# Fused attention and two mixture products on one core: a planner that orders the stage, and a power of two moved onto x

## The chip, the cores and the metric

The kernel runs on one core of a Trainium2 chip. The metric is the device time of one execution in microseconds (us); all times here are microseconds unless marked ns. The engines are PE (matrix products, with PEld for the loading of its weights), DVE (vector), ACT (activations), POOL (GpSimd) and SP (which issues most transfers). "Clock" is the clock that was granted to PE, as a share of its 2.4 GHz.

## What is computed

Causal attention on 2 batches x 12 heads, 448 positions, width 64; its output, laid out as 896 tokens x 768, goes through a gated product (w_a and w_b 768 x 1536, w_out 1536 x 768) and then through one of eight experts per token (768 x 1024 x 768):

```python
scores = scale * np.matmul(q, k.transpose(0, 1, 3, 2))
mask = np.triu(np.ones((seq, seq), dtype=bool), k=1)
scores = np.where(mask, -1000000000.0, scores)
scores = scores - np.max(scores, axis=-1, keepdims=True)
attn = np.exp(scores)
attn = attn / (np.sum(attn, axis=-1, keepdims=True) + 1e-09)
return np.matmul(attn, v).astype(np.float32)
...
x = np.ascontiguousarray(attn_out.transpose(0, 2, 1, 3)).reshape(B * S, H * D)
...
a = x @ w_a
b = x @ w_b
return (a * b @ w_out).astype(np.float32)
...
logits = xn @ en.T / tau
expert_idx = np.argmax(logits, axis=1)
...
h = np.maximum(x[mask] @ w1[e], 0.0)
out[mask] = gate_w[mask, None] * (h @ w2[e])
```

## The kernel before

Heads are taken in twelve pairs (six per batch, `pairs`). Of a pair the scores come in three units (`UNITS`: rows 336 to 447, rows 112 to 223, and the other two chunks), and five steps (`SUBS`) turn them into products with V. Of each step `exps` (L373, ACT) makes the exponentials and their sums from the scores and the maxima (`maxima`, L357, DVE), `turn` (L382, PE) transposes the probabilities, `p_hi` (L385, ACT) and `p_lo` (L388, DVE) split them into two float16 halves in one of `NTB = 3` buffers `tbuf`, and `pv` (L404 to L406, PE) multiplies them by V's halves. After a pair `inverse` (L415) and `weigh` (L428, DVE) divide by the sums into x0, and then `turn_x` (L449, PE) and `halves_x` (L455 ACT, L457 DVE) make the pair's part of x's halves. `prep` scales K and V on POOL (L304, L307), copies V's high half on ACT (L310) and makes its low half on POOL (L313).

The weights arrive as float64. A conversion makes one block of 128 x 768 into two float16 halves: `a`, `b`, `c` (L218, L222, L226, DVE), `e` (L232, ACT) and `d` (L236, DVE); there are 24 blocks of w_a and w_b and 12 of w_out, the first eight of them in attention. A block of w_out is also transposed by a transfer (`we_turn`) and multiplied with the embedding on PE (`we_mm`, L615 and L616).

The first product (`gemm1_steps`, L517 to L519) goes in units of one block f of 128 columns and one batch hf: 18 matmuls of 448 columns for a and 18 for b, 24 units, 864 matmuls. The result of a is multiplied on DVE by `rows` (L525), then by b (L529); ACT makes the high half of g (L530), POOL the low one (L531). `rows` is a power of two per token, made from the squared norms of x0 (`squares`, `norm`), spread over the partitions by a product with ones (`spread`, L495) and copied (L498). The second product (L839) follows.

What sets the order: each engine runs its instructions in program order, and the program is written by a list of tasks, each put at a step and with a rank inside it:

```python
    def at(step, rank, fn):
        lst = tasks.setdefault(max(step, clock[0]), [])
        lst.append((rank, len(lst), fn))
...
    for g in range(NU):
        at(S0 + g, 3, lambda g=g: exps(g))
        at(S0 + g + 1, 1, lambda g=g: turn(g))
        at(S0 + g + 1, 3.2, lambda g=g: p_hi(g))
        at(S0 + g + 2, 1.5, lambda g=g: p_lo(g))
        at(S0 + g + 2, 8, lambda g=g: pv(g))
    for s in range(S0 + 5 * NSB, S0 + NU):
        at(s, 9, lambda s=s: fill(FILL))
    FILL = 3
    for s in range(S0 + NU):
        if s < 4 or s % 5 in (0, 2):
            at(s, 9.3, tick)
```

Step g thus has its exponentials in one slot, its transposes and high half in the next, its low half and its products in the one after; within a slot the rank decides. `fill` writes up to three times three matmuls of the first product, if the conversion and the part of x that they need have been written, and `tick` one instruction of a conversion. The loads of a pair (`load`) are written two pairs ahead, those of the weights (`more_raw`) one after each conversion, all on SP's queue. The units that `fill` could reach are those of blocks 0 to 3 with batch 0 and of block 0 with batch 1; the others come after attention, in the same way by steps, with one instruction of a conversion to two groups of three matmuls.

## Time and profile before

| | us |
|---|---|
| runs before: median (lowest to highest of 3) | 672.51 (669.19 to 676.47) |
| the profiled execution, its own time | 676.15 |
| its span, first to last instruction | 674.4 |
| PE busy over the span | 570.2 (85%) |
| DVE, ACT, POOL busy | 416.9 (62%), 202.5 (30%), 153.0 (23%) |

All durations come from that one profiled execution. Matmuls are pipelined and their ends are modelled, so a matmul's own duration is longer than its share of PE: what a row of matmuls costs is read from the starts. "Idle before" is the time for which an engine had nothing to run before such an instruction, with what ended it.

### The profile page before, as it was taken

The numbers are of one execution on the slowest core, as the hardware profiler recorded it, in microseconds if no ns is written. First come the engines' busy times: TensorE is split into PE (matmuls) and PEld (weight loads), VectorE is DVE, ScalarE is ACT, GpSimd is POOL, SyncE is SP. The second block draws the span as 40 slices with busy tenths as digits, with TensorE's granted clock in tenths as the row PEclk, the third lists the DMA queues.
The fourth block names the chain that finished last, engine by engine and source line by source line (L and its number), as shares of the span: only waits on it lengthen the run. The fifth ranks groups of instructions, "written<-read, shape, count | busy, mean of one in ns | idle before, by whom it ended". The sixth has DMA issues, their size and how long they took to land. (4 is left out here: it accounts for less than half of the span.)

```text
span 674.4 us, 12613 instructions
## 1 busy us (share of the span) xinstructions
PE 570.2 (85%) x5102; PEld 378.8 (56%) x5102; DVE 416.9 (62%) x643; ACT 202.5 (30%) x465; POOL 153.0 (23%) x134
## 2 busy tenths in 40 slices
PE   2767787787988699999998599999599879998994
PEld 1545554454655355455544266665588675957772
DVE  3865555634455389877998506888448974959100
ACT  2554445523446322222222100110312133322221
POOL 5422222202331022121111000000133334334222
PEclk9976566578979699999999699999999999999998
DMA  8430321202010056524799303988487884857111
GB/s 303 156 104 15 96 81 40 89 28 88 15 48 1 1 80 204 185 93 134 186 256 199 70 2 133 319 299 286 105 193 219 296 264 129 273 181 243 39 34 29
DMA packets 46230, 93.04 MB, mean 138 GB/s; under 512 B 23430, under 2 KB 26502, under 8 KB 46160
## 3 DMA queue, kind: packets, MB, share of 16 engines
q1 hardware_dynamic: 43872, 84.16, 41.8%
q0 software_dynamic: 2288, 7.91, 3.5%
q8 instruction: 48, 0.79, 0.5%
q14 instruction: 22, 0.18, 0.1%
HBM read 79.46 MB, written 9.05 MB: 131 GB/s over the span
## 5 line engine op out<-in xcount | busy, mean ns | idle before, releaser
L517 PE MATMUL ab<-bufA 128*128 128x448 f16 x288 | 105.3, 365 | 9.6 <-DVE asb L525 4.9
L518 PE MATMUL ab<-bufA 128*128 128x448 f16 x288 | 105.6, 366 | 0.0
L519 PE MATMUL ab<-bufA 128*128 128x448 f16 x288 | 105.4, 366 | 0.0
L357 DVE TENSOR_REDUCE mn<-sc 112x2 f32<-112x896 f32 (+3 forms) x48 | 34.4, 737 | 65.6 <-PE sc L346 65.6
L382 PE MATMUL pt<-id,pr 112*112 112x112 f32 x240 | 44.8, 325 | 32.3 <-DVE tbuf L388 16.5
L839 PE MATMUL x<-woc,gL 128*128 128x512 f16 x336 | 57.4, 326 | 0.0
L385 ACT ACTIVATE tbuf<-pt 112x448 f16<-112x448 f32 x60 | 32.6, 543 | 79.7 <-PE pt L382 68.0
L373 ACT ACTIVATE pr<-sc,mn 112x336 f32<-112x336 f32 (+2 forms) x96 | 46.6, 492 | 26.5 <-DVE mn L357 20.7
L382 PEld LDWEIGHTS pt<-id,pr 112*112 112x112 f32 x240 | 32.2, 168 | 39.2 <-issue 27.3
L340 PE MATMUL sc<-ld,ld 64*112 64x448 f32 (+3 forms) x192 | 45.2, 582 | 5.8 <-POOL ld L304 5.8
L518 PEld LDWEIGHTS <-bufA 128*128 128x128 f16 x288 | 28.9, 100 | 36.1 <-issue 14.0
L519 PEld LDWEIGHTS <-bufA 128*128 128x128 f16 x288 | 29.1, 101 | 28.6 <-issue 3.6
L388 DVE TENSOR_TENSOR tbuf<-pt,tbuf 112x448 f16<-112x448 f32 x60 | 36.7, 612 | 11.6 <-ACT tbuf L385 11.6
L839 PEld LDWEIGHTS <-gL 128*128 128x128 f16 x336 | 32.1, 98 | 20.5
L517 PEld LDWEIGHTS <-bufA 128*128 128x128 f16 x288 | 29.1, 101 | 25.2 <-issue 2.8
L406 PE MATMUL po<-vh,tbuf 112*128 112x64 f16 x240 | 34.9, 216 | 9.4 <-DVE tbuf L388 7.4
L531 POOL TENSOR_TENSOR gL<-asb,gL 128x448 f16<-128x448 f32 x16 | 20.6, 1290 | 94.6 <-ACT gL L530 94.6
L1041 PEld LDWEIGHTS <-hh 128*128 128x128 f16 x320 | 30.9, 98 | 19.8
L226 DVE SCALAR_TENSOR_TENSOR cv<-raw,cv 128x768 uint32<-128x768 uint32 x36 | 40.9, 1136 | 0.5
L222 DVE SCALAR_TENSOR_TENSOR cv<-raw,cv 128x768 uint32<-128x768 uint32 x36 | 37.7, 1047 | 0.7
L313 POOL TENSOR_TENSOR vl<-ld,vh 112x512 f16<-112x512 f32 x12 | 15.1, 1259 | 95.7 <-ACT vh L310 95.7
L404 PE MATMUL po<-vh,tbuf 112*128 112x64 f16 x240 | 36.7, 219 | 0.1
(229 smaller groups left out, 1388.1 us busy)
## 6 DMA issues: line engine op xcount, KB each, us to landing
rw<-in_moe_w_dram SPq DMA_DIRECT2D x36, 512.0 KB, 6.2
rw<-in_moe_w_dram SPq DMA_DIRECT2D x48, 384.0 KB, 5.3
raw<-in_moe_w_a_dram SPq DMA_DIRECT2D x12, 768.0 KB, 7.2
raw<-in_moe_w_b_dram SPq DMA_DIRECT2D x12, 768.0 KB, 6.4
raw<-in_moe_w_out_dram SPq DMA_DIRECT2D x12, 768.0 KB, 4.7
ld<-in_k_dram SPq DMA_DIRECT2D x12, 224.0 KB, 2.5
ld<-in_q_dram SPq DMA_DIRECT2D x12, 224.0 KB, 2.8
ld<-in_v_dram SPq DMA_DIRECT2D x12, 224.0 KB, 2.5
```

Of the source, the lines that this page charges most:

```text
L222: nc.vector.scalar_tensor_tensor(t, r()[:, :, 1], 0xC0000000, t, op0=ALU.bitwise_and, op1=ALU.bitwise_or)
L226: nc.vector.scalar_tensor_tensor(t, r()[:, :, 0], 29, t, op0=ALU.logical_shift_right, op1=ALU.bitwise_or)
L340: nc.tensor.matmul(sc[:CP, j, o : o + W], qt[hd, c * CP : W], kt[hd, :W], start=n == 0, stop=False)
L373: nc.scalar.activation(pr[:, d : d + W], sc[:CP, jj, o : o + W], AF.Exp, bias=mn[:, c, jj : jj + 1], scale=-1.0, accum_out=sums[pi][:, c, ...
L382: nc.tensor.transpose(pt[:CP, cs], prs[g][:, cs], id32[:CP, :CP])
L388: nc.vector.tensor_tensor(tbufs[g % NTB][:, 1, :S], pts.pop(g)[:CP, :S], tbufs[g % NTB][:, 0, :S], op=ALU.subtract)
L404: nc.tensor.matmul(po[:, c, jj, :], ph, vh[:, kc, jj, :], start=kc == 0, stop=False)
L406: nc.tensor.matmul(po[:, c, jj, :], pl_, vh[:, kc, jj, :], start=False, stop=kc == c)
L517: nc.tensor.matmul(o, w[:, 0, i, kc, :], xTh[:, kc, ts], start=kc == 0, stop=False)
L518: nc.tensor.matmul(o, w[:, 0, i, kc, :], xTl[:, kc, ts], start=False, stop=False)
L519: nc.tensor.matmul(o, w[:, 1, i, kc, :], xTh[:, kc, ts], start=False, stop=kc == KC - 1)
L839: nc.tensor.matmul(xp[:, ns], G(f)[:, a, tk], woc[:, f, l, ns], start=st, stop=sp)
```

## The change

The list of steps is replaced by a planner (`Plan`). Each piece of work becomes an `op` with an engine, an estimated duration, the pieces that it needs and a rank. The planner keeps an estimated clock for each engine; it picks, for the engine that can start first, the piece of lowest rank among those that can start within a small slack, adds its estimated duration, and writes the instruction. The kernel holds the order that comes out; nothing is decided while it runs. It covers all from the first K to the last block of w_out; the 36 matmuls of a unit are now single pieces of rank 5000, after everything in attention.

The power of two per token no longer comes in as `rows`. `norm` makes it as before from the squares of x0, now for exponents in steps of two, and `x_scale` multiplies x0 by it, two chunks on ACT and two on DVE, when all six pairs of a batch are weighed. Only then is x turned, six times for a batch in a row (`turn_x` by batch and block), instead of once after every pair. Gone are `rows`, its product with ones, its copy, and the multiplication by it: `g_a` is now a scaled copy on ACT. `g_lo` moves from POOL to DVE, `v_hi` from ACT to POOL, the first half of the reciprocal (`inverse`) from DVE to POOL, pair 0's K scaling from POOL to DVE. Buffers: probabilities and `tbuf` four instead of three, conversions three instead of two, x0 two instead of one. Only pair 0's loads stand ahead of the set-up now. The first eight conversions wait, in the plan, for the exponentials of steps 20, 25, ... 55, so that the first stands in the fifth pair.

```diff
+class Plan:
+    SLACK = {"PE": 0.1, "DVE": 0.2, "ACT": 0.1, "POOL": 0.0, "SP": 0.0}
+    LAT = {"PE": 0.3, "DVE": 0.17, "ACT": 0.2, "POOL": 0.2, "SP": 2.2}
...
+    def pick(self, eng):
+        t, best = self.free[eng], None
+        for o in self.wait[eng]:
+            r = t
+            for d in o.deps:
+                if d.end is None:
+                    break
+                r = max(r, d.end + (d.lat if d.eng != eng else 0.0))
+            else:
+                key = (0, o.rank, r) if r <= t + self.SLACK[eng] else (1, r, o.rank)
+                if best is None or key < best[0]:
+                    best = (key, r, o)
+        return best
...
+        oa = op("DVE", 0.6, a, ld, old(NCV, 5), after, rank=k)
...
+        eng = nc.vector if pi == 0 else nc.gpsimd
+        eng.tensor_scalar(ldt[pi, 1], ldt[pi, 1], SQ, None, op0=ALU.mult)
...
+        nc.gpsimd.tensor_copy(vf(qkv[pi][0]), vf(ldt[pi, 2]))
...
-        nc.vector.tensor_scalar(rs, rs, 1e-9, SV, op0=ALU.add, op1=ALU.mult)
+        nc.gpsimd.tensor_scalar(rs, rs, 1e-9, SV, op0=ALU.add, op1=ALU.mult)
...
+    def x_scale(b, c):
+        x0 = x0s[b][:, c, :]
+        if c % 2:
+            nc.vector.tensor_scalar(x0, x0, r2[b][:, c : c + 1], None, op0=ALU.mult)
+        else:
+            nc.scalar.activation(x0, x0, AF.Copy, scale=r2[b][:, c : c + 1])
...
-                at(c + 1, 1.8, lambda: nc.vector.tensor_tensor(asb, rows[:, hf, :], o, op=ALU.mult))
...
-                at(c + 2, 4, lambda: nc.gpsimd.tensor_tensor(G(f)[:, 1, ts], asb, G(f)[:, 0, ts], op=ALU.subtract))
...
+        nc.scalar.activation(asb, gt[0][:, :S], AF.Copy, scale=ACU)
...
+        nc.vector.tensor_tensor(G(f)[:, 1, ts], gt.pop(("a", f, hf)), G(f)[:, 0, ts], op=ALU.subtract)
...
+    for i, fn in enumerate(emb_tasks):
+        emb_o = op("DVE", 0.2, fn, emb_o, rank=12 + 0.01 * i)
...
+                t_o[g] = op("PE", 0.4, lambda g=g: turn(g), e_o[g], l_o.get(g - 2), rank=g + 0.5)
+                h = op("ACT", ACTC(S), lambda g=g: p_hi(g), t_o[g], v_o.get(g - NTB), rank=g + 0.6)
+                l_o[g] = op("DVE", DVEC(S), lambda g=g: p_lo(g), h, rank=g + 0.6)
+                v_o[g] = op("PE", 0.37, lambda g=g: pv(g), l_o[g], vl_o[pi], wg_o.get(pi - 1), v_o.get(g - 1), rank=g + 1.5)
...
+                    prev_mm[0] = op("PE", 0.189, lambda f=f, hf=hf, i=i, kc=kc, n=n: mm(f, hf, i, kc, n), *deps, rank=5000)
...
+    for n in range(NC1):
+        conv_ops(n, after=e_o[C1A + C1B * n])
...
+    for f in range(NF):
+        conv_ops(2 * NF + f)
+        to = op("SP", 2.0, lambda f=f: we_turn(f), conv[2 * NF + f][5], we_o.get(f - NWT), rank=400)
+        we_o[f] = op("PE", 0.4, lambda f=f: we_mm(f), to, rank=400)
```

How the order of the instructions changes is shown at three places. The first is the start of DVE's queue: cv is a block under conversion, mn the maxima, gE and esm the embedding and its norms. Before:

```order
L137 CAST idb<-id_96 112x112
L139 CAST id_103<-id_96 128x128
L218 TENSOR_SCALAR cv_170<-raw_168 128x768
L222 SCALAR_TENSOR_TENSOR cv_170<-raw_168,cv_170 128x768
L226 SCALAR_TENSOR_TENSOR cv_170<-raw_168,cv_170 128x768
L357 TENSOR_REDUCE mn_184<-sc_179 112x2
L218 TENSOR_SCALAR cv_191<-raw_172 128x768
L236 SCALAR_TENSOR_TENSOR bufA<-cv_170,bufA 128x768
```

After, the last steps of the embedding's chain, which starts DVE's queue, and what stands behind it:

```order
L299 TENSOR_SCALAR esm<-esm 8x1
L302 TENSOR_SCALAR esm<-esm 8x1
L303 RECIPROCAL esm<-esm 8x1
L333 TENSOR_SCALAR ld_0_84<-ld_0_84 128x448
L304 TENSOR_SCALAR gE<-gE,esm 8x768
L305 RECIPROCAL rtau<-rtau 128x1
L378 TENSOR_REDUCE mn_174<-sc_159 112x2
L378 TENSOR_REDUCE mn_174<-sc_169 112x2
```

The conversion that stood ahead of the first maxima is gone, and the whole chain on the embedding, with the scaling of pair 0's K (ld_0) in it, stands there now.

The second place is DVE in the fifth pair before (pt are transposed probabilities, x_0 the output of batch 0, px turned x):

```order
L415 TENSOR_SCALAR sums_668<-sums_668 112x8
L420 RECIPROCAL rr_843<-sums_668 112x8
L218 TENSOR_SCALAR cv_858<-raw_189 128x768
L388 TENSOR_TENSOR tbuf_115<-pt_826,tbuf_115 112x448
L428 TENSOR_TENSOR x_0_390<-po_744,rr_843 112x4x128
L388 TENSOR_TENSOR tbuf_117<-pt_860,tbuf_117 112x448
L357 TENSOR_REDUCE mn_779<-sc_891 112x2 x2
L222 SCALAR_TENSOR_TENSOR cv_858<-raw_189,cv_858 128x768
L388 TENSOR_TENSOR tbuf_113<-pt_884,tbuf_113 112x448
L357 TENSOR_REDUCE mn_941<-sc_931 112x2
L457 SCALAR_TENSOR_TENSOR bufA<-px_919,bufA 128x448
```

and in the fourth and fifth pair after:

```order
L378 TENSOR_REDUCE mn_729<-sc_750 112x2
L409 TENSOR_TENSOR tbuf_111<-pt_745,tbuf_111 112x448
L258 TENSOR_SCALAR cv_797<-raw_192 128x768
L262 SCALAR_TENSOR_TENSOR cv_797<-raw_192,cv_797 128x768
L409 TENSOR_TENSOR tbuf_113<-pt_778,tbuf_113 112x448
L378 TENSOR_REDUCE mn_729<-sc_788 112x2 x2
L409 TENSOR_TENSOR tbuf_107<-pt_815,tbuf_107 112x448
L447 TENSOR_TENSOR x_0_395<-po_709,rr_761 112x4x128
L378 TENSOR_REDUCE mn_862<-sc_821 112x2
L409 TENSOR_TENSOR tbuf_109<-pt_844,tbuf_109 112x448
L409 TENSOR_TENSOR tbuf_111<-pt_856,tbuf_111 112x448
```

The low halves of turned x (L457) no longer stand among a pair's work, the first half of the reciprocal (L415) has gone to POOL, and the first conversion begins here.

The third place is PE after the last product with V (pn is the spread row factor, ab a result of the first product). Before:

```order
L406 LDWEIGHTS tbuf_117
L406 MATMUL po_2214<-vh_165,tbuf_117 128x64
L449 MATMUL px_2322<-id_96,x_1_1418 128x112 x4
L495 LDWEIGHTS onesb
L495 MATMUL pn_2339<-dg_142,onesb 128x112
```

After:

```order
L507 LDWEIGHTS bufA
L507 MATMUL ab_2151<-bufA 128x448
L461 MATMUL px_2174<-id_90,x_1_1358 128x112 x8
L461 MATMUL px_2185<-id_90,x_1_1358 128x112 x8
L507 LDWEIGHTS bufA
```

Before, the turned x and the row factor follow at once on the last product with V, and then come 705 matmuls of the first product. After, 29 of its matmuls stand between that product and the turned x, and 796 behind them; 39 stand ahead of it, where 159 stood.

## Rows read from the trace of the kernel before

**Rows 1.** Busy time by stage: width, busy (instructions) of PE, PEld, DVE, ACT, POOL; clock; DMA

```profile
14.82:116.34 101.52, 75.79 (x672) 52.84 (x673) 62.70 (x116) 52.06 (x158) 29.16 (x21) 0.75 0.28 89
116.34:224.10 107.76, 88.81 (x779) 58.51 (x777) 55.34 (x104) 49.80 (x148) 21.13 (x16) 0.81 0.13 42
224.10:236.60 12.50, 7.56 (x31) 3.26 (x28) 3.73 (x12) 2.18 (x8) 0.00 (x0) 0.59 0.01 1
236.60:375.80 139.20, 134.07 (x806) 70.03 (x805) 122.06 (x149) 33.69 (x47) 26.95 (x21) 1.00 0.62 165
```

**Rows 2.** In order of time, three places: start, duration, engine, line, names, idle before

```profile
14.82 0.62 ACT L373 ACTIVATE pr<-sc,mn 112x448 f32<-112x448 f32 x1
...
224.08 0.19 PE L406 MATMUL po<-vh,tbuf 112*128 112x64 f16 x1
...
384.17 5.29 PE L839 MATMUL x<-woc,gE 128*128 128x512 f16 x24
```

**Rows 3.** Groups of DVE until 240: busy, mean ns, idle before and who ended it

```profile
L388 DVE TENSOR_TENSOR tbuf<-pt,tbuf 112x448 f16<-112x448 f32 x60 | 36.7, 612 | 11.6 <-ACT tbuf L385 11.6
L357 DVE TENSOR_REDUCE mn<-sc 112x2 f32<-112x896 f32 (+3 forms) x48 | 34.4, 737 | 65.6 <-PE sc L346 65.6
```

**Rows 4.** PE in order of time, 199.6 to 201.9

```profile
199.64 0.55 PE L382 MATMUL pt<-id,pr 112*112 112x112 f32 x4
200.11 1.02 PE L340 MATMUL sc<-ld,ld 64*112 64x336 f32 x8
...
201.31 0.19 PE L404 MATMUL po<-vh,tbuf 112*128 112x64 f16 x1
...
201.66 0.36 PE L517 MATMUL ab<-bufA 128*128 128x448 f16 x1
201.85 0.35 PE L518 MATMUL ab<-bufA 128*128 128x448 f16 x1
```

**Rows 5.** PE in order of time, 73.7 to 76.6

```profile
73.72 0.26 PE L404 MATMUL po<-vh,tbuf 112*128 112x64 f16 x1
...
74.38 0.97 PE L382 MATMUL pt<-id,pr 112*112 112x112 f32 x4
75.28 1.09 PE L340 MATMUL sc<-ld,ld 64*112 64x224 f32 x4
...
76.53 0.26 PE L404 MATMUL po<-vh,tbuf 112*128 112x64 f16 x1
```

**Rows 6.** In order of time: the transfer and first step of the embedding

```profile
2.99 0.75 POOL L176 DMA_DIRECT2D gE<-in_moe_expert_emb_dram  x1
...
15.78 1.91 DVE L261 SCALAR_TENSOR_TENSOR gE<-gE 8x768 f32<-8x768 f32 x1
```

**Rows 7.** DMA issues: KB each, median us from issue to landing

```profile
gE<-in_moe_expert_emb_dram POOLq DMA_DIRECT2D x1, 24.0 KB, 6.0
```

**Rows 8.** Lines of the conversion: duration ns min/median/max, first and last start

```profile
L218 DVE TENSOR_SCALAR cv<-raw x36: 506/550/1424, 11.0 to 373.1; 128x768 uint32<-128x768 uint32 x36
...
L222 DVE SCALAR_TENSOR_TENSOR cv<-raw,cv x36: 906/959/1794, 11.6 to 375.5; 128x768 uint32<-128x768 uint32 x36
...
L226 DVE SCALAR_TENSOR_TENSOR cv<-raw,cv x36: 906/951/1676, 12.6 to 376.5; 128x768 uint32<-128x768 uint32 x36
...
L236 DVE SCALAR_TENSOR_TENSOR bufA<-cv,bufA x24: 934/950/1782, 14.9 to 323.7; 128x768 f16<-128x768 f32 x24
```

**Rows 9.** Groups of PE from 224.1 to 384.1

```profile
L517 PE MATMUL ab<-bufA 128*128 128x448 f16 x235 | 84.1, 358 | 1.2 <-DVE asb L525 1.1
L615 PE MATMUL pW<-en,woT 128*128 128x16 f16 x71 | 5.1, 171 | 12.1 <-DMA woT<-woc 12.1
```

**Rows 10.** In order of time: a POOL subtraction and a conversion beside it

```profile
238.87 1.67 POOL L531 TENSOR_TENSOR gE<-asb,gE 128x448 f16<-128x448 f32 x1 [27.16 <-ACT gE L530]
...
239.68 1.67 DVE L226 SCALAR_TENSOR_TENSOR cv<-raw,cv 128x768 uint32<-128x768 uint32 x1
```

**Rows 11.** Groups of DVE in the dense stage, 236.6 to 375.8

```profile
L226 DVE SCALAR_TENSOR_TENSOR cv<-raw,cv 128x768 uint32<-128x768 uint32 x27 | 31.4, 1165 | 0.4
```

More of the change, by code (lines that the diff above doesn't have):

```diff
@@ L128, in load @@
         ldt[pi, i] = t
-    for pi in range(2):
-        for i in (1, 0, 2):
-            load(pi, i)
+    for i in (1, 0, 2):
+        load(0, i)
     id32 = cst.tile([P, P], F32, name="id32")
@@ L236, in d @@
             nc.vector.scalar_tensor_tensor(lo, st["t"].bitcast(F32), SW, hi, op0=ALU.mult, op1=ALU.subtract)
[L237 to L254 removed]
+        old = lambda k, i: conv[n - k][i] if n >= k else None
+        k = 1000 + n
+        ld = op("SP", 2.6, lambda: ab_raw(n), old(NRAW, 3), old(1, 0), rank=k)
+        oa = op("DVE", 0.6, a, ld, old(NCV, 5), after, rank=k)
+        ob = op("DVE", 0.88, b, oa, rank=k)
+        oc = op("DVE", 0.88, c, ob, rank=k)
+        oe = op("ACT", 0.75, e, oc, *dest_free, rank=k)
+        od = op("DVE", 0.88, d, oe, rank=k - 0.5)
+        conv[n] = (ld, oa, ob, oc, oe, od)
     esm = cst.tile([E, 4], F32, name="esm")
@@ L433, in weigh @@
-        at(s0 + 1, 4.7, lambda: halves_x(pi, 1))
-        if hp >= NPR - 2:
-            part = hp - NPR + 2
-            for c in range(NCH):
-                at(s0 + 1 + (0 if part else c), 5.2, lambda c=c: squares(b, c, part))
-        if hp == NPR - 1:
-            at(s0 + 2, 5, lambda: norm(b))
-            at(s0 + 3, 9.2, lambda: spread(b))
-            at(s0 + 4, 3.5, lambda: spread_done(b))
-    pxs = {}
-    def turn_x(pi):
-        b, hp = pairs[pi]
-        pxs[pi] = pt = psA.tile([P, 512], F32, tag="pt", name=f"px{pi}", bufs=2)
-        for c in range(NCH):
-            nc.tensor.transpose(pt[:, c * CP : (c + 1) * CP], x0s[b][:, c, 2 * hp * D : (2 * hp + 2) * D], id32[:CP, :CP])
@@ new lines, in ACTC, with DVEC, last @@
+    def ACTC(n):
+        return 0.09 + 0.00084 * n
+    def DVEC(n):
+        return 0.08 + 0.00104 * n
+    ld_, sc_o, e_o, t_o, v_o, l_o, x_o = {}, {}, {}, {}, {}, {}, {}
+    ac_free, sc_free = [], []
+    def last(lst, k):
+        return lst[-k] if len(lst) >= k else ()
+    emb_o = None
+    for i, fn in enumerate(emb_tasks):
+        emb_o = op("DVE", 0.2, fn, emb_o, rank=12 + 0.01 * i)
+    eo = op("PE", 0.5, emb_turn, emb_o, rank=13)
+    eh = op("ACT", 0.3, emb_hi, eo, rank=13)
+    el = op("DVE", 0.25, emb_lo, eh, rank=13)
@@ new lines, in fused_kernel @@
+    seq = [(f, hf) for hf in range(2) for f in range(4)] + [(f, hf) for f in range(4, NF) for hf in range(2)]
+    for n in range(NC1):
+        conv_ops(n, after=e_o[C1A + C1B * n])
+    for f in range(NFIRST):
+        unit(f, 0)
+    plan.run(needed)
+    begun = [x for x in unit_o if unit_o[x][0].end is not None]
+    for x in unit_o:
+        if x not in begun:
+            plan.drop(unit_o[x])
+    plan.run([o for x in begun for o in unit_o[x]])
+    prev_mm[0] = mm_o[begun[-1]] if begun else None
@@ L585, in fused_kernel @@
+    prev_lo[:] = [unit_o[x][-1] for x in begun]
     psx.close()
@@ L618, in fused_kernel @@
     wo_buf["c"] = woc
-    steps = []
-    for f in range(1, 4):
-        steps += gemm1_steps(f, 1)
-    for f in range(4, NF):
-        steps += gemm1_steps(f, 0) + gemm1_steps(f, 1)
-    for n in range(0, len(steps), 2):
-        for st in steps[n : n + 2]:
-            at(clock[0], 6, st[1])
-        if n % 12 != 10:
-            at(clock[0], 9, lambda n=n: tick())
-        run_step()
-    while conv:
-        at(clock[0], 9, tick)
-        run_step()
-    while tasks and max(tasks) >= clock[0]:
-        run_step()
+    del ac_free[:]
+    for f, hf in seq[len(begun) :]:
+        for i in range(2):
+            if 2 * f + i not in conv:
+                conv_ops(2 * f + i, mm_o[f - NS, 1] if f >= NS else None)
+        unit(f, hf)
+    we_o = {}
+    for f in range(NF):
+        conv_ops(2 * NF + f)
+        to = op("SP", 2.0, lambda f=f: we_turn(f), conv[2 * NF + f][5], we_o.get(f - NWT), rank=400)
+        we_o[f] = op("PE", 0.4, lambda f=f: we_mm(f), to, rank=400)
+    plan.run([o for e in plan.wait for o in plan.wait[e]])
     cvs.close()
```

329 lines of the change are left out of this document (161 added, 168 removed).

## The prediction

> **What bounds the kernel now.** I read the busy time by stage first, then the groups of the attention stage, then PE in order of time. By stage the span splits into attention (first scores of exponentials at 14.82 to the last product with V at 224.1), a short join, the dense first product, a tail, and the second product from 384.17 on, which the change leaves alone [rows 1, 2]. In attention no engine is full: PE shows 76 and 89 of 102 and 108 us, DVE 63 and 55, ACT 52 and 50 [rows 1]. The time goes into engines waiting for each other: the maxima on DVE waited 65.6 us for PE's scores [rows 3]. The twelve pairs of heads took (224.1 - 14.82) / 12 = 17.4 us each. PE's granted clock was 0.75 and 0.81 there, that is, it went between its two levels. The dense stage is PE's: 134 of 139 us at clock 1.00 [rows 1].
>
> What a pair costs PE when nothing waits is read from starts in a row. At the higher level (2.4 GHz): four transposes 0.47 (199.64 to 200.11), scores of the third unit 1.20 (200.11 to 201.31), a product with V 0.35 (201.31 to 201.66) [rows 4]; the first unit has as many columns with half the mask matmuls, an estimated 1.1. At the lower level (1.2 GHz): product 0.66, transposes 0.90, scores of the second unit 1.25 [rows 5]; the first two are about 1.85 times the higher level's, so the second unit is some 0.70 there. A pair is 5 x 0.47 + 1.20 + 1.1 + 0.70 + 5 x 0.35 = 7.1 us at the higher level and 7.1 x 1.85 = 13.1 at the lower.
>
> **The change, part by part.**
>
> *Start.* The K scaling of pair 0 goes from POOL to DVE, and there it stands behind the whole chain on the expert embedding. That chain waits for a transfer that POOL issues at 2.99 [rows 6] and that lands 6.0 us later [rows 7], at about 9.0. Behind it are queued the scaling, and for it PE's first scores, and the first maxima. Sum: 9.0 + 1.9 for the squares of the embedding [rows 6] + 14 small steps at an estimated 0.17 + 0.5 for the scaling + 2.2 for the first scores (1.20 x 1.85) + 1.1 for the maxima = 17.1 instead of 14.82: 2.3 us lost. If the squares take less and the transfer lands at 7, it is nothing; if the transfer is delayed by the other loads, 5.
>
> *Attention, pairs 0 to 3.* The conversions now begin with the twenty-first step (pair 4), and the turned x with pair 6. DVE has left per pair 34.4 / 12 = 2.9 for maxima, 5 x 0.612 for the low halves [rows 3], and an estimated 0.9 for weighing and reciprocal: 6.9 us. ACT had 52.06 / 6 = 8.7 per pair [rows 1] and loses V's copy (to POOL) and x's half, each an activation of some 0.6 like the one at 14.82 [rows 2]: about 7.5. PE needs 7.1 or 13.1. So no engine needs more than 7.5 at the higher level, and PE alone sets 13.1 at the lower. The planner's order is what fills the waits: instead of one fixed slot per step an engine gets whatever is ready by estimate, and four buffers stand behind the probabilities and their halves instead of three. I take 10.1, the middle between 7.1 and 13.1, since the granted clock before was itself midway (0.75).
>
> *Attention, pairs 4 to 11.* Eight conversions fall here, one per pair. Alone one is 0.51 + 0.91 + 0.91 + 0.95 = 3.3 us on DVE by the shortest instances [rows 8]. To 6.9 + 3.3 come about 1.0 per pair for six low halves of x, its scaling, the norms and one and a half units of the first product: 11.2. PE at the lower level needs 13.1 + (six turned x at 0.9 + 39 matmuls at 2 x 0.189) / 8 = 15.6. The middle is 13.4. V's high half on POOL costs POOL at most another 1.6 per pair (what a POOL instruction of that shape takes is bounded by its other two, nothing at the low end if ACT was the tighter); POOL was busy 29.2 / 6 = 4.9 of 17 per pair [rows 1], so it fits. The reciprocal's first half now waits in POOL's queue too, behind such an instruction for 0 to 1.6 us, and the weighing, and with it the next pair's products, wait with it; four buffers cover this, so I take 0 and leave 12 x 1.6 = 19 in the upper end. On SP the weights' loads stand between the pairs' loads, each behind an earlier conversion; three Ks and Qs are loaded ahead, which hides that. The last product with V then comes at 17.1 + 4 x 10.1 + 8 x 13.4 = 164.7 instead of 224.1.
>
> *First product.* By the order 159 of its 864 matmuls stood before the last product with V, leaving 705 (235 at each of three lines) [rows 9]; now 39 do, leaving 825, so 120 more at the 0.189 that two starts in a row show (201.66, 201.85) [rows 4]: 22.7 us that before lay inside attention. 825 x 0.189 = 155.9. With it 24 turned x (6 x 0.47 = 2.8) and twelve small products with the turned output weights at about 0.3 (3.6): 162.3. The join shrinks: before, PE did 7.6 us of work in 12.5 at clock 0.59 [rows 1]; now 29 matmuls of the first batch (5.5 us) stand between the last product with V and the first turned x, beside weighing, squares, norm and scaling (0.7 + 2 + 0.9 + 1.7 = 5.3 estimated from the like instructions). So the row factor's broadcast and its waits go, and nothing new shows if the units run ready; if not, 5 us.
>
> *DVE and POOL in the dense stage.* The row factor's multiplication goes to ACT as a scaled copy, the low half of g comes from POOL to DVE: two DVE instructions per unit as before. But the conversions get quicker. Beside a POOL subtraction of 1.67 one of them took 1.67 [rows 10], where the shortest took 0.91 and the median 0.95 [rows 8]. The mean in this stretch was 1.17 [rows 11]; with no POOL work beside, 28 conversions at 3.4 and 23 units at 1.2 are 123 us of DVE in 162: PE stays the bound. The Trainium skill says why in "SBUF — State Buffer", section "Who interferes with whom": a DVE instruction with two SBUF inputs and a GpSimd one that reads SBUF block each other for the whole instruction. The trace agrees (1.67 against 0.91); by that rule the gain is DVE's alone here and the sum stays, while V's copies on POOL give some of it back in attention.
>
> *Tail.* Before, PE waited 12.1 us for turned output weights, mostly after its last unit [rows 9]. Now 42 matmuls (7.9 us) stand behind the last of these small products. Conversion and transfer of the twelve blocks go one behind another; before they came 4.8 us apart, and DVE needs 3.4 + 0.8 now. I take 6 of the 12.1 us as left, and 2 us for the change of the PSUM pool; ends 0 and 15. Dense stage: 162.3 + 8 = 170.3, against 384.17 - 224.1 = 160.1.
>
> **Sum.** Second product from 164.7 + 170.3 = 335.0 instead of 384.2: 49 us earlier. The rest of the span (290 us) keeps its instructions. The profiled execution took 676.15 us (span 674.4), 3.6 above the median of the runs shown, 672.5; 676.15 - 49 = 627, and on the median's footing 672.5 - 49 = 623.5, which I round to 624.
>
> A rule that speaks against it: the Trainium skill, "Perfetto Trace Analysis", section "Optimization Strategy", says that stages with different limits may gain by being interleaved, and this change takes 120 matmuls out of such a mixture. The trace bears it out in part: the second batch held most of the 159 and took only 6.2 us longer than the first [rows 1]. By that the sum would be some 18 us better had they stayed; it holds their full 22.7.
>
> **The rivals.**
> *PE at its lower level all through attention.* For it: with transposes, narrow products and waits the clock of 0.75 came about although PE showed 75 to 82% busy [rows 1]. Against it: the waits that the planner closes are PE's. Time: 17.1 + 4 x 13.1 + 8 x 15.6 = 194.3, the second product at 364.6, 652 us. Chance 0.18.
> *PE at its higher level, DVE and ACT bound.* 17.1 + 4 x 7.5 + 8 x 11.2 = 136.7; with the dense stage without waits at 162.3 + 2, second product at 301, 589 us. For it: in the stretch of [rows 4] PE ran without a gap at that level. Chance 0.17.
> *Slower: the order is fixed by estimates, and one late engine holds all.* The place is PE's queue in attention: a transpose whose exponentials are late stands ahead of everything else. If a pair takes 17.4 us as now, the last product with V comes at 226, the 120 matmuls come on top, second product at 396, 684 us. It decides from (384.2 - 170.3 - 17.1) / 12 = 16.4 us a pair. For it: estimated durations that hold at the higher level only. Against it: even all of attention at the lower level is 14.8. Chance 0.10, of which slower by over 1% 0.06.
> Mine, the mixture: 0.55.
>
> **How the numbers follow.** The time is the mixture's 624. Its own range is 605 to 642; to both sides it reaches to the rivals, leaving half of each out: 597 to 654. One per cent is about what a measurement here can tell from no change. Faster by more: 0.55 + 0.17 + 0.17 of the lower level's 0.18 = 0.89; within: 0.05; slower: 0.06.
>
> **What would show it.** Right: first exponentials near 17; a pair every 10, then 13 us; granted clock above 0.8 in attention; the last product with V near 165; PE without a gap at 0.189 a matmul after that; conversions at 0.91 to 0.96; the second product near 335. Wrong: pairs of over 16 us, or PE waiting for DVE in the dense stage for more than 15 us in all, or the first exponentials after 22.

## The result, and the profile after

The changed kernel takes 585.81 us (median of 4 runs, 585.13 to 586.54) against 670.85 for the kernel before (median of 4, 669.1 to 676.47) in the same session: 0.872 of the time, 95% interval 0.8664 to 0.8776. The forecast was 624 with a range of 597 to 654, so the time lies 38 us below the forecast and 11 below the range. It is the rival "PE at its higher level, DVE and ACT bound" that came nearest (589, given 0.17). The profiled execution before, 676.15, is one of the slower runs, 5.3 above that median, so a difference taken from its trace can be too large by as much.

| | before | forecast | after |
|---|---|---|---|
| first exponentials | 14.82 | 17.1 | 17.31 |
| last product with V | 224.1 | 164.7 | 126.65 |
| second product starts | 384.17 | 335.0 | 294.86 |
| span behind that | 290.2 | 290.2 | 289.8 |
| profiled execution, own time (span) | 676.15 (674.4) | | 586.54 (584.7) |

Three of the four stages came out as worked. The start is 0.2 us from the forecast. From the last product with V to the second product it is 168.2 us, against 170.3 worked out and 160.1 before. The rest is unchanged. All of the error is in attention: 147.6 us forecast, 109.3 measured, 38 less.

Two of the three milestones of the changed kernel in order of time (start, duration, engine, line, names), which answer [rows 2]:

```profile
17.31 0.63 ACT L394 ACTIVATE pr<-sc,mn 112x448 f32<-112x448 f32 x1 [15.23 <-DVE mn L378]
...
126.65 0.19 PE L427 MATMUL po<-vh,tbuf 112*128 112x64 f16 x1
```

and the third, the group of the second product on PE, with its first and last start behind the durations:

```profile
L893 PE MATMUL x<-woc,gE x168: 272/326/379, 294.9 to 374.3; 128*128 128x512 f16 x84, 128*128 128x256 f16 x84
```

Busy time by stage (width; busy and instructions of PE, PEld, DVE, ACT, POOL; clock; DMA), in the order first half of attention, second half, join, dense stage, which answers [rows 1]:

```profile
17.31:69.40 52.09, 48.05 (x636) 35.25 (x635) 43.40 (x74) 42.81 (x140) 30.91 (x30) 1.00 0.47 142
69.40:126.60 57.20, 52.42 (x671) 38.58 (x670) 55.00 (x96) 49.01 (x152) 23.31 (x22) 0.97 0.30 96
126.60:138.90 12.30, 10.03 (x71) 6.09 (x68) 11.17 (x22) 9.35 (x23) 1.19 (x1) 1.00 0.31 114
138.90:294.86 155.96, 153.22 (x933) 80.32 (x931) 117.50 (x159) 46.53 (x73) 0.99 (x1) 1.00 0.57 157
```

Read the clock column first. It was 0.75 and 0.81 in the two halves of attention [rows 1]; now it is 1.00 and 0.97, the higher level (2.4 GHz) nearly throughout. The column does not show the first pair's start: four transposes at 21.31 took 0.95 us and those at 23.95 took 0.57, so the lower level lasted until about 23. Then PE against the width: 44.7 us of attention were empty on PE before (209.28 less 164.60, row below), now 8.8 (109.35 less 100.52). And DVE is 55.00 of 57.20 us busy in the second half: there it is at its limit, as the rival said. In the first half it is not: PE, with 48.05 of 52.09, is the fullest there.

Attention as a whole, first exponentials to last product with V, of the kernel before and of the changed one:

```profile
14.82:224.10 209.28, 164.60 (x1449) 111.34 (x1449) 118.03 (x219) 101.86 (x306) 50.29 (x37) 0.78 0.20 65
```

```profile
17.31:126.66 109.35, 100.52 (x1307) 73.89 (x1307) 98.45 (x169) 91.88 (x290) 54.22 (x51) 0.98 0.38 118
```

So the 99.9 us that attention lost are 35.9 of PE's empty time and 64.1 of its busy time. Of the busy time 22.7 are the 120 matmuls that stand behind attention now (120 x 0.189, and they came back there); the other 41 are in the main the same instructions at the higher clock (by the counts above, 22 other instructions of PE went too).

The groups of the page that answer [rows 3] (busy, mean ns, idle before and who ended it):

```profile
L409 DVE TENSOR_TENSOR tbuf<-pt,tbuf 112x448 f16<-112x448 f32 x60 | 36.1, 618 | 4.6 <-ACT tbuf L406 4.5
L378 DVE TENSOR_REDUCE mn<-sc 112x2 f32<-112x896 f32 (+3 forms) x48 | 34.3, 734 | 5.6 <-PE sc L367 5.5
```

The two kinds of instruction cost the same as before (612 and 737 ns there); the maxima's wait for scores went from 65.6 to 5.6 us.

What PE waited for in attention before (who waits, for whom, us in total, times, longest), a view that the prediction did not read, and the same of the changed kernel:

```profile
PE pt L382 <- DVE tbuf L388: 16.5, 9, 2.4
PE pt L382 <- DVE bufA L457: 8.4, 7, 1.4
PE po L406 <- DVE tbuf L388: 7.4, 8, 1.8
PE pt L382 <- ACT pr L373: 6.2, 1, 6.2
```

```profile
PE po L427 <- DVE tbuf L409: 7.9, 11, 3.3
PE sc L361 <- ACT pr L394: 0.4, 2, 0.2
```

The first two rows before are one thing. L382 turns probabilities into one of two PSUM banks named pt, and it waited for DVE to empty such a bank: of the low half of the probabilities (L388), or of the low half of x (L457), since the turned x of each pair was put into a pt bank as well. In the changed kernel x is turned once per batch, and not into pt; these waits are gone.

### The profile page after: what moved, and what is told of

Same layout as the page of the kernel before. It is cut to its first block, busy times and chain, and to the rows that moved or that the text cites. A ratio compares the mean times of both kernels' runs of the same rounds, so it can differ in the third digit from the quotient of the medians.

```text
span 584.7 us, 12576 instructions
## 1 busy us (share of the span) xinstructions
PE 529.2 (90%) x5094; PEld 356.6 (61%) x5094; DVE 401.9 (69%) x628; ACT 210.8 (36%) x487; POOL 138.3 (24%) x134
## 5 line engine op out<-in xcount | busy, mean ns | idle before, releaser
L507 PE MATMUL ab<-bufA 128*128 128x448 f16 x864 | 168.0, 352 | 2.4 <-ACT asb L511 1.8
L361 PE MATMUL sc<-ld,ld 64*112 64x448 f32 (+3 forms) x192 | 34.8, 463 | 14.5 <-DVE ld L333 14.0
L1081 POOL TENSOR_TENSOR hl<-hr,hh 128x512 f16<-128x512 f32 x20 | 26.7, 1333 | 46.7 <-ACT hr L1080 38.8
L515 DVE TENSOR_TENSOR asb<-asb,ab 128x448 f32<-128x448 f32 x24 | 14.9, 619 | 32.8 <-PE ab L507 31.5
L406 ACT ACTIVATE tbuf<-pt 112x448 f16<-112x448 f32 x60 | 32.0, 544 | 13.8 <-PE pt L403 13.4
L1098 ACT ACTIVATE y<-py,sc 128x512 f32<-128x512 f32 (+1 forms) x20 | 10.5, 577 | 71.9 <-DMA sc<-xsc,gidi 27.0
L872 DVE TENSOR_SCALAR bufC<-rw 128x768 f16<-128x768 f32 (+1 forms) x28 | 20.0, 713 | 21.8 <-DMA rw<-in_moe_w_dram 15.6
L427 PE MATMUL po<-vh,tbuf 112*128 112x64 f16 x240 | 27.4, 194 | 7.9 <-DVE tbuf L409 7.9
L876 DVE SCALAR_TENSOR_TENSOR bufC<-rw,bufC 128x768 f16<-128x768 f32 (+1 forms) x28 | 32.6, 1163 | 1.4
L876 DVE SCALAR_TENSOR_TENSOR bufB<-rw,bufB 128x768 f16<-128x768 f32 (+1 forms) x28 | 32.4, 1158 | 1.3
L876 DVE SCALAR_TENSOR_TENSOR bufA<-rw,bufA 128x768 f16<-128x768 f32 (+1 forms) x28 | 30.0, 1073 | 1.3
```

Source lines behind the costliest of these rows:

```text
L361: nc.tensor.matmul(sc[:CP, j, o : o + W], qt[hd, c * CP : W], kt[hd, :W], start=n == 0, stop=False)
L406: nc.scalar.activation(tbufs[g % NTB][:, 0, :S], pts[g][:CP, :S], AF.Copy)
L507: nc.tensor.matmul(gt[i][:, :S], w[:, h, i, kc, :], x[:, kc, ts], start=kc == n == 0, stop=kc == KC - 1 and n == 2)
L876: nc.vector.scalar_tensor_tensor(dl, R.pop(("raw", j, pc))[:, :n], SE, dh, op0=ALU.mult, op1=ALU.subtract)
```

## The experiments

The first theory was: the planner's free choice on PE took away its waits, and without waits the clock stayed up. The rival: the other parts of the change did it.

**PE back to a fixed order, throughout, then in attention alone.**

```
-    SLACK = {"PE": 0.1, ...
+    SLACK = {"PE": 1e6, ...
```

> The changed kernel, but PE takes its attention work by the fixed ranks (the lowest rank whose inputs are already placed), instead of what is ready by estimate; DVE, ACT and POOL are still planned, and buffers, conversions and V's copies stay as changed. Theory (the free choice on PE removed its waits, and with the waits gone the granted clock rose to 1.00): waits return, the clock in attention falls below 0.90, the last weighing comes after 145 instead of 127.6, total 605 to 645. Rival (the gain is that of the other parts: later conversions, fewer matmuls in attention, four buffers): last weighing before 132, clock at 0.97 or more, total 582 to 592.

Measured: last weighing at 130.4, clock 0.97 in attention, but 634.32 us. The first two numbers are the rival's; the total lies in the theory's 605 to 645, but not for the theory's reason. PE's waits behind attention show it:

```profile
PE pW L673 <- DMA woT<-woc: 35.5, 12, 4.1
PE ab L507 <- ACT asb L511: 1.7, 1, 1.7
```

By rank the small products with the turned output weights (L673, rank 400) stood ahead of the matmuls (rank 5000), and PE waited 35.5 us for their transfers. The edit was too wide; the second run keeps it to attention.

```
+    plan.SLACK = dict(Plan.SLACK, PE=1e6)
     plan.run(needed)
+    plan.SLACK = Plan.SLACK
```

> The changed kernel, PE by the fixed ranks in attention alone; from the last product on by the planner's free choice as before the edit, so that the matmuls of the dense stage no longer stand behind the small products with the turned output weights. Theory (the free choice on PE is worth nothing in attention, the 48 us of the run with fixed ranks throughout came from the dense stage): total 585 to 597, the most of it the 39 matmuls that now follow attention (39 x 0.19 = 7.4). Rival (it costs in attention too, and what ended at 130.4 was paid for behind it): 600 to 630.

Measured: 592.27 us in one run, attention 110.8 (16.9 to 127.7) at clock 0.98. The free choice on PE is worth at most 1.5 us in attention; of the 6.5 us in all most are the 29 of the 39 matmuls that now follow attention (29 x 0.189 = 5.5). My first theory falls in the part that named PE's order. In the dense stage it is worth most of the 42 us between the two runs (35.5 us is PE's wait).

**The fourth buffer.** `NTB = NPB = 3` instead of 4.

> The changed kernel with three buffers instead of four for the probabilities and for their halves, planned with that. Theory (the order matters, the fourth buffer little): 584 to 592. Rival (the fourth buffer is what lets the planner fill waits): 600 or more, with PE or ACT waiting in attention and the clock below 0.95.

Measured: 584.26 us (583.2 to 585.38), ratio to before 0.8716, 0.8628 to 0.8804: the same as with four. The fourth buffer is worth nothing that can be measured here.

**One pt bank instead of two in the changed kernel.**

```
-    ... tag="pt", name=f"pt{g}", bufs=2)
+    ... tag="pt", name=f"pt{g}", bufs=1)
-    t_o[g] = op("PE", 0.4, lambda g=g: turn(g), e_o[g], l_o.get(g - 2), rank=g + 0.5)
+    t_o[g] = op("PE", 0.4, lambda g=g: turn(g), e_o[g], l_o.get(g - 1), rank=g + 0.5)
```

> The changed kernel with one PSUM buffer instead of two for the turned probabilities, planned with that: each turn waits for the low half of the step before, a chain of about 0.54 (ACT) + 0.62 (DVE) + some 0.4 of signalling = 1.5 us in which PE has only scores and products to do. The kinds and numbers of PE's instructions stay the same. Theory (waits bring the clock down): PE's idle time in attention rises from 8.8 to 30 us or more, the granted clock falls below 0.95, total 615 to 650. Rival (the clock follows the kinds of instruction, waits do not touch it): the same idle time but a clock of 0.98 as now and 0.47 for four turns; total 605 to 625.

Measured: 649.99 us; attention:

```profile
17.60:207.60 190.00, 151.80 (x1411) 101.13 (x1411) 114.39 (x184) 100.31 (x301) 49.17 (x51) 0.79 0.24 79
```

Empty time on PE 38.2 us, clock 0.79: one bank less gives the planned kernel the clock of the kernel before, and nearly its length. The kinds of instruction are the same (and 144 matmuls of the first product fall inside the longer stretch, for 39). So it is not the kinds of instruction, transposes and narrow products, that bring the clock down: the same ones ran at 0.98 without this wait chain. The Trainium skill, "TensorE: Matmul & The Clock Gate", section "A second HAM failure mode: psum-queue depth-cycling", tells of a kernel in which PE idles briefly between groups while it cycles through PSUM banks, and whose clock swings between its levels. The row agrees: 0.79 with one bank, 0.98 with two.

How much PE waits does not set the clock, though. PE was empty 21% of attention in the kernel before, at 0.78, and 20% here, at 0.79; it was also empty 20% of two stretches of the kernel before with other edits (shown below), and there the clock was 0.94 and 1.00. Which waits lower the clock, and which do not, no run here tells.

**The kernel before, mended wait by wait.** The next six runs, one execution each and on several chips, go the other way: the fixed steps stay, and one cause after another is taken out. Attention is compared by its length; totals are given beside those of the kernel before on the same chip. First, no matmuls of the first product in attention, and later conversions:

```
-    FILL = 3
+    FILL = 0
-        if s < 4 or s % 5 in (0, 2):
+        if s >= 25 and s % 5 < 4:
...
-        if clock[0] >= S0 + NU:
-            at(clock[0], 6, lambda: fill(3))
```

> The kernel before, with one part of the change alone: no matmul of the first product in attention (they follow it), and the conversions begin with the twenty-sixth step, four ticks in five steps. Theory (the fixed steps make the waits): attention stays above 180 us (it was 209, of which 159 matmuls at 0.19 to 0.35 are 30 to 55), granted clock at most 0.80 there, total 655 to 690. Rival (the gain came from taking matmuls and early conversions out of attention): attention at 150 us or less, total 600 to 625.

Measured: 679.74 us (672.35 before on that chip), attention 185.6 at clock 0.72. The rival falls: the waits are in the steps themselves. Then x in a bank of its own, on top of that:

```
-        pxs[pi] = pt = psA.tile([P, 512], F32, tag="pt", name=f"px{pi}", bufs=2)
+        pxs[pi] = pt = acc(f"px{pi}")
```

> The kernel of the run with no matmuls in attention (679.7), with one edit more: the turned x of each pair goes to the bank that the first product's accumulator has, instead of taking one of the two banks of the turned probabilities. In the two traces before it, PE's turns wait 16.5 and 16.2 us for a low half and 8.4 and 12.7 us for the half of x, that is for these two banks; after the change they wait 0.1. Theory (the shared banks made most of the waits, and the waits the lower clock): attention falls from 185.6 to 150 us or less, granted clock there from 0.72 to 0.88 or more, total 640 or less. Rival (DVE's fixed order made them, maxima that wait for scores ahead of low halves): attention 168 us or more, total 660 to 680.

Measured: 651.9 us (669.22 before), attention 153.2. The turns no longer wait (1.7 us in all for a bank), but products with V do, for low halves:

```profile
PE po L406 <- DVE tbuf L388: 36.4, 26, 3.2
```

The mechanism is the theory's (attention 32.4 us shorter, the clock from 0.72 to 0.88); the sizes fell short of it, by 3 us in attention and 12 in the total. The other suspect alone, in the untouched kernel before, matmuls and all:

```
-            at(s0 + n, 4, lambda pi=pi, u=u: maxima(pi, u))
+            at(s0 + n + 1, 1.6, lambda pi=pi, u=u: maxima(pi, u))
```

> The kernel before with one edit: each maximum on DVE stands one step later, behind the next low half, instead of in the step of its scores. Theory (shared banks): attention stays above 185 us (209 before), total 650 to 676. Rival (DVE's order with maxima ahead of low halves, where they waited 65.6 us for scores): attention 165 us or less, maxima's wait below 30 us, total 600 to 630.

Measured: 634.78 us beside 669.22 for the kernel before on that chip, attention 169.7 at clock 0.94, between the two forecasts of attention, and the total between those of the total. DVE's wait for scores:

```profile
L357 DVE TENSOR_REDUCE mn<-sc 112x2 f32<-112x896 f32 (+3 forms) x48 | 34.0, 728 | 0.6 <-PE sc L346 0.5
```

Attention as a whole, and PE's longest waits in it:

```profile
15.90:185.60 169.70, 136.32 (x1448) 93.50 (x1449) 121.67 (x218) 100.31 (x305) 50.22 (x37) 0.94 0.24 79
```

```profile
PE pt L382 <- DVE bufA L457: 11.0, 7, 2.7
PE po L406 <- DVE tbuf L388: 10.3, 14, 1.7
PE pt L382 <- ACT pr L373: 8.6, 3, 7.2
PE pt L382 <- DVE tbuf L388: 3.5, 6, 1.3
```

One line of the fixed order is worth 34 us. A maximum that waits on DVE for its scores holds the low half queued behind it, and that half is what PE's products, and the pt bank, wait for: PE's wait for a pt bank that a low half holds fell from 16.5 to 3.5 us. I had read the 65.6 us [rows 3] as idle time of an engine that was not full. Both edits together, without matmuls in attention:

> The kernel before with both edits of the two runs on it, on top of no matmuls in attention: the turned x in a bank of its own, and each maximum one step later. With the bank alone attention took 153.2 us and PE's waits there were nearly all products waiting for low halves (36.4); with the maxima alone, and the 159 matmuls inside, 169.7 us. Theory (these two waits were what held the fixed steps, the planner only happens to have neither): the 36.4 us go nearly whole, attention 112 to 130, granted clock 0.95 or more, total 610 to 628. Rival (fixed slots bring new waits in their place): attention 140 or more, total 638 or more.

Measured: 643.38 us (671.51 before), attention 147.9, clock 0.87. The rival: new waits took their place, and a pair took 10.5 us at clock 1.00 until the conversions began (weighings at 21.08 to 52.54), then 13.1 at 0.81 (to 157.47):

```profile
21.08:52.54 31.46, 25.20 (x338) 18.48 (x337) 24.38 (x51) 22.68 (x73) 14.67 (x12) 1.00 0.25 74
```

The two edits do not add up. The bank alone shortened attention by 32.4 us and the later maxima alone by 39.6 (209.3 to 169.7); the maxima on top of the bank gave 5.3 (153.2 to 147.9). They are for the most part two ways out of the same loss. The conversions were taken out as well:

```
-        if s >= 25 and s % 5 < 4:
+        if s >= 1000:
...
     while fillers:
+        at(clock[0], 9.3, tick)
```

> The kernel before with the turned x in its own bank and maxima one step later, and no conversions in attention either: all of them follow it. With conversions from step 25 a pair took 10.3 us at a clock of 1.00 until they began and 13.1 at 0.82 after that. Theory (conversions in fixed slots, ahead of low halves that are ready later, are the third wait): every pair at 10.3 us or a little over, attention 120 to 128, clock 0.97 or more all through. Rival (the fixed slots decay by themselves, or x's halves behind ACT do it): the later pairs still at 12 us or more, attention 140 or more, clock below 0.90. The total says nothing here, since eight to ten conversions then stand between attention and the first product.

Measured: 632.55 us (665.8 before on that chip), attention 127.9, clock 0.92. The conversions in fixed slots cost 20 us of attention. Length and pairs are the theory's; the clock stayed below its 0.97. A pair took 10.6 us on average then (20.94 to 137.40), 9.8 at the best. DVE still waited ahead of low halves, once in every pair, this time for ACT's half of x:

```profile
DVE bufA L457 <- ACT bufA L455: 23.6, 12, 2.1
```

So DVE's low half of x goes one step later too:

```
-        at(s0 + 1, 4.7, lambda: halves_x(pi, 1))
+        at(s0 + 2, 1.7, lambda: halves_x(pi, 1))
```

> The run before it on the kernel before (632.6: x in its own bank, maxima later, no conversions in attention), and one edit more: DVE's low half of x stands one step later too, where ACT has had a whole step for the high half. DVE waited there 23.6 us, twelve times, ahead of low halves that the products wait for (20.4 us on PE). Theory (every such wait ahead of a low half is what the fixed order loses, the third is this one): DVE's wait below 5 us, attention from 127.9 to 108 to 118, granted clock 0.95 or more, total 612 to 624. Rival (fixed slots are the limit): attention 124 or more, total 628 or more.

Measured: 626.09 us (675.1 before on that chip), attention 124.9, clock 0.95; that wait fell from 23.6 to 0.9, and attention by 3.0 only, since DVE now waits for the half that it works on itself:

```profile
DVE tbuf L388 <- ACT tbuf L385: 24.7, 27, 1.7
```

In attention the rival holds (124 or more); the total lies between the two. The attention windows of these runs, in the order no matmuls; own bank; both edits; no conversions; x's half later:

```profile
9.20:194.80 185.60, 137.43 (x1290) 97.82 (x1290) 116.20 (x214) 100.60 (x302) 43.93 (x33) 0.72 0.25 86
```

```profile
9.20:162.40 153.20, 111.03 (x1291) 83.21 (x1291) 114.63 (x214) 99.64 (x302) 44.76 (x33) 0.88 0.31 104
```

```profile
9.20:157.10 147.90, 113.49 (x1290) 83.33 (x1290) 116.47 (x214) 98.38 (x302) 45.11 (x33) 0.87 0.32 108
```

```profile
9.20:137.10 127.90, 104.56 (x1291) 77.56 (x1291) 92.37 (x182) 92.01 (x294) 43.93 (x34) 0.92 0.23 76
```

```profile
9.20:134.10 124.90, 104.81 (x1291) 76.08 (x1291) 95.53 (x182) 91.25 (x294) 43.08 (x33) 0.95 0.24 77
```

Look at width, PE and clock together: the same 1290 or 1291 instructions on PE, 137 us busy at 0.72 and 105 at 0.95, and 48 us empty at the top, 20 at the bottom. The planner's 109.35 holds 39 matmuls and most of eight conversions besides. What sets the last 16 us between them was not settled: no run puts the planner's order of DVE and ACT, step by step, into the fixed slots, none puts the maxima ahead of the low halves in the planner, and none takes back alone the move of V's copies and of the reciprocal to POOL.

**The rank of the conversions in the planner.**

```
         k = 1000 + n
         ld = op("SP", 2.6, lambda: ab_raw(n), old(NRAW, 3), old(1, 0), rank=k)
+        k = n - 1000 if n < NC1 else k
         oa = op("DVE", 0.6, a, ld, old(NCV, 5), after, rank=k)
```

> The changed kernel with the eight conversions in attention ranked ahead of everything on DVE and ACT instead of behind everything: the planner then places them as soon as they are free to start, and low halves wait up to 0.95 us for each of their four instructions. Theory (what conversions cost lies in what they stand ahead of): PE's waits for low halves rise from 7.9 to 15 us or more, attention 116 to 130 instead of 110, total 591 to 612. Rival (the planner hides them at either rank, since all costs are known to it): 583 to 589.

Measured: 590.77 us in one run, the last weighing at 137.2 instead of 127.6 and attention 120.4, inside the theory's 116 to 130; yet PE waited 8.2 us for low halves, as before the edit (7.9). The total lies between the two forecasts, and the waits that the theory named did not come. Inconclusive; about 5 us in this one run.

**No matmuls in attention in the changed kernel.** `NFIRST` 0 instead of 4.

> The changed kernel without matmuls of the first product in attention: the 39 that stood there follow it, 39 x 0.189 = 7.4 us more in the dense stage. Theory (DVE sets the later pairs, PE had the room for them): attention keeps its length, total 590 to 595. Rival (PE, 92% busy in attention, sets the pace, a matmul costs the same in either place): 584 to 588.

Measured: 601.19 us (599.63 to 603.31), 15.4 more than the changed kernel. Both forecasts were too low, since they left out that the edit also empties the join: besides the 39 in attention, 33 matmuls stood in it (126.68 to 138.0). 72 x 0.189 = 13.6 us. The join:

```profile
129.00:147.00 18.00, 10.07 (x39) 6.28 (x40) 16.16 (x29) 8.76 (x20) 2.17 (x2) 0.53 0.61 120
```

With matmuls to do, PE worked through the join at clock 1.00 (10.03 of 12.30 us). With none it waited 5.0 us for the scaled x, and its clock was 0.53 for 18 us. The traces tell the parts apart. Attention took 112.4 us instead of 109.4, so it kept nearly its length, as the theory said, and won nothing by losing the matmuls. From its last product with V to the second product it is 184.9 us (128.6 to 313.5) instead of 168.2: of these 16.7 the 39 matmuls are 7.4, and the other 9.3 go with the emptied join: its first matmul of the product starts only at 142.17, and the first 31 take 8.0 us, where 31 x 0.189 is 5.9.

**The low half of g on POOL again.** `nc.gpsimd` for `nc.vector` in `g_lo`, planned so.

> The changed kernel with the low half of g on POOL again, as before the change. In the dense stage DVE loses 23 x 0.62 = 14 us, and its conversions run beside POOL's subtractions. Theory (PE sets the dense stage whatever DVE does): the mean of the conversions' two-input instructions rises from 0.95 to 0.99 to 1.10 or more, total 583 to 589. Rival (DVE is near enough the bound for the slower conversions to show): 592 or more.

Measured: 585.11 us (584.46 to 587.18): no change, PE is the bound. Only one of the three two-input conversions got slower; without and with POOL's subtraction, dense stage:

```profile
L266 DVE SCALAR_TENSOR_TENSOR cv<-raw,cv 128x768 uint32<-128x768 uint32 x29 | 27.7, 955 | 0.5
L262 DVE SCALAR_TENSOR_TENSOR cv<-raw,cv 128x768 uint32<-128x768 uint32 x28 | 26.8, 958 | 0.9
L273 DVE SCALAR_TENSOR_TENSOR bufA<-cv,bufA 128x768 f16<-128x768 f32 x17 | 16.0, 954 | 0.9 <-ACT bufA L269 0.9
```

```profile
L266 DVE SCALAR_TENSOR_TENSOR cv<-raw,cv 128x768 uint32<-128x768 uint32 x28 | 27.5, 980 | 0.6
L262 DVE SCALAR_TENSOR_TENSOR cv<-raw,cv 128x768 uint32<-128x768 uint32 x28 | 26.8, 956 | 0.8
L273 DVE SCALAR_TENSOR_TENSOR bufA<-cv,bufA 128x768 f16<-128x768 f32 x17 | 19.5, 1167 | 0.0
```

L273 went from 954 to 1167 ns, the other two stayed: one of the three pays beside POOL's subtractions, and here PE hides it.

**K's scaling first.** The embedding chain is created with pair 1, behind the exponentials of pair 0.

```
-    emb_o = None
-    for i, fn in enumerate(emb_tasks):
-        emb_o = op("DVE", 0.2, fn, emb_o, rank=12 + 0.01 * i)
...
+        if pi == 1:
+            emb_o = e_o[NSB * pi - 1]
+            for i, fn in enumerate(emb_tasks):
+                emb_o = op("DVE", 0.2, fn, emb_o, rank=r0 + 7 + 0.01 * i)
...
```

> The changed kernel with the chain on the expert embedding placed behind the exponentials of pair 0 instead of ahead of pair 0's K scaling on DVE. K and Q of pair 0 land at about 6.3 and 7.4 us; then 0.4 for the scaling, 2.3 for the first scores, 1.1 for the maxima: first exponentials at about 11 instead of 17.3. Theory (this start is on the path, nothing later waits for a transfer instead): 6 us less, 578 to 582. Rival (the loads of the next pairs, or DVE's work in pairs 1 and 2, take it back): 584 to 587.

Measured: 577.6 us (576.18 to 579.24), ratio to before 0.8646 (0.8575 to 0.8717), 8.2 us under the changed kernel, with ranges that do not meet. K's scaling starts at 3.4 instead of 13.53, the first exponentials at 7.4 (11 was forecast), the last weighing at 122.0. Of the 9.9 us won at the start attention gave back 4.2 (113.6 us instead of 109.4). This version beats both kernels. The conversions begun earlier on top of it (`C1A, C1B` 5, 6 instead of 20, 5):

> The run with K's scaling first (577.6), with the eight early conversions begun at step 5 and then every six steps, instead of at step 20 and every five. DVE was 31 of 34 and 39.4 of 40 us busy in the second half of attention and 32 of 40.6 in the first. Theory (DVE sets the second half and has room in the first): 4 to 8 us less, 569 to 574. Rival (PE, 37.7 of 40.6 busy in the first half, or the transfers of weights beside those of K, Q and V there, take it back): 576 to 581.

Measured: 577.54 us (575.47 to 580.37), no change, as the rival said: attention took 115.7 us instead of 113.6. Which of the rival's two causes it was, no run tells.

## Why the prediction was wrong

- **Start:** right, 17.31 against 17.1, by the steps named (the squares at 9.03, the scaling at 13.53). What I did not ask is whether the queue could be left: 8.2 us of the total lay there.
- **Pairs 0 to 3, the step that failed:** "I take 10.1, the middle between 7.1 and 13.1, since the granted clock before was itself midway (0.75)". From the first weighing at 30.63 to the fourth at 54.37 a pair took 7.9 us, clock 1.00. The lower end was nearly right and the choice of the middle was not: a clock that belonged to the old order and its waits was carried over to a kernel without them. One bank less brings 0.79 back in the changed kernel; the bank alone lifts the kernel before without matmuls in attention from 0.72 to 0.88. In the sum this step made little: 40.4 us were taken for the four pairs and 37.1 measured (17.31 to 54.37), since the first pair alone took 13.3, a start that the sum had no term for.
- **Pairs 4 to 11, the same step:** 13.4 was taken, 9.2 measured (54.37 to 127.62), at clock 0.98. Here lie 35 of the 38 us: 107.2 taken to the last product with V, 72.3 measured. Half of it is the middle (13.4 for 11.2). The other half is the lower end itself, 11.2 of DVE, which was too high: DVE was busy 70.5 us there, 8.8 a pair. Of these 2.4 us a pair the conversions explain 0.7: six of the eight, not all, fell inside, and they took 20.8 us, 2.6 a pair for 3.3. About 1.0 is that durations were added up as if one began when the other ended. The groups of DVE in this stretch sum to 78.9 us for 70.5 busy, because a duration can reach into the next one:

```profile
57.03 0.95 DVE L266 SCALAR_TENSOR_TENSOR cv<-raw,cv 128x768 uint32<-128x768 uint32 x1
57.89 0.55 DVE L258 TENSOR_SCALAR cv<-raw 128x768 uint32<-128x768 uint32 x1
```

- **What fills the waits:** "an engine gets whatever is ready by estimate, and four buffers stand behind the probabilities" named the wrong parts. PE's choice and the fourth buffer are worth next to nothing in attention. What held the kernel before was DVE's queue (maxima ahead of low halves, x's low half, conversions) and the two pt banks; taken out by hand these bring its attention to 124.9 us, and the last 16 stay open. The prediction quoted the 65.6 us and never asked what was queued behind them. That x now leaves the pt banks alone, I had not counted as a part of the change at all.
- **Dense stage and tail:** right, 168.2 against 170.3. PE was empty 5.0 us from 126.6 to the second product, where 8 were taken; the wait for turned output weights, 6 taken, was 1.8, and PE's waits for ACT and DVE behind attention were 3.1 together. No row shows the 2 us for the change of the PSUM pool by itself. The conversions ran at 954 to 958 ns there, inside the 0.91 to 0.96 forecast.
- **Interleaving:** that the time would be 18 us better had the 120 matmuls stayed was not tried. The run without any matmuls shows the other side of it: the 72 that stand in attention and the join take 13.6 us, and without them there the time is 15.4 us longer, so in those places they run for nothing.
- **Rivals:** the lower level all through (652) and the one late engine (684) found nothing in the trace. The rival that came was worked as 589 and deserved more than 0.17: the row that speaks for it was quoted [rows 4]. That its total is only 3 us off is partly luck: it had 30.0 and 89.6 us for the two groups of pairs, where 37.1 and 72.3 were measured, and 164.3 for the dense stage against 168.2.
- **Two slips in the sums:** the starts in [rows 5] give 1.9, not 1.85, between the levels (0.66 to 0.35, 0.90 to 0.47), and the lower level's total is 653 by its own terms (672.5 less 384.2 - 364.6). Neither moves the forecast by more than about 2 us.

## What to carry to other kernels

When an in-order engine shows long idle time before one group, ask what is queued behind the waiting instruction and who waits for that; moving the waiting one a step later was worth 34 us in a kernel in which no engine was full in that stage (PE 79%, DVE 56% busy). A granted clock between the two levels belonged here to an order and its waits, not to the kinds of instruction, so a change that removes the waits is better priced at the higher level, with the lower as the rival; how much waiting the higher level stands, these runs do not tell. And keep independent matmuls for the waits inside a stage and for the join behind it: in this kernel they cost nothing there.

## What the runs showed that I had not expected

The fixed order lost time twice, in the waits and in the clock: with the same 1290 or 1291 instructions PE was 137.43 us busy at clock 0.72 and 104.81 at 0.95. The amount of waiting alone does not say which clock is granted: PE was empty a fifth of the time at 0.78, 0.79, 0.94 and 1.00. Two PSUM banks against one, for a tile of 112x448, decide 64 us in the planned kernel (649.99 against 585.81), while a fourth buffer of the same data in SBUF decides nothing (584.26 with three). The Trainium skill, "Perfetto Trace Analysis", section "Optimization Strategy", says that the same gap repeating on the engine that should be full can mean too little SBUF or PSUM for the next tile. Here PSUM was a part of it, and the run with three SBUF buffers shows that in the changed kernel the fourth of them was not.
